# Exponentials of four slots in one instruction, their exponents formed by TensorE from split halves and scaled identities; the carry moved from the forward transform into the kernel spectrum

## The chip, the cores and the metric

One Trainium2 chip, one of its cores. The metric is the device time of the slowest (here the only) core in microseconds, lower is better. "Time" is that of a whole run; "span" is the length of one profiled execution, about 1.8 us less in the two profiled runs (171.17 and 169.4 before, 176.92 and 175.1 after). The engines are called PE (TensorE), DVE (VectorE), ACT (ScalarE), POOL (GpSimd) and SP (SyncE, which only issues transfers here). In the profile's names `AR` is the on-chip working memory (SBUF) and `ps` is PSUM, the memory into which PE writes its products; an evacuation is the copy of such products from PSUM to SBUF. u is the input, F1 the first of four forward matrices, `eye` and `rest` two parts of the constants. The granted clock is the share of full speed that the profile shows TensorE to have been given.

## The reference, cut to what matters

```python
def reference(A_u, ..., gate_w):
    g = sigmoid((x * gate_w).sum(-1, keepdims=True))
    a = _A_ref(x, ...)          # long convolution, 512 channels of 2048 steps
    b = _B_ref(x, ...)          # two routed rows through a small gated MLP
    return g * a + (1 - g) * b

def _A_ref(u, A_re, A_im, B_re, B_im, C_re, C_im, log_dt, Dskip):
    dt = exp(log_dt)[:, None]
    logdA = dt * (A_re + 1j * A_im)                     # 512 x 128
    P = exp(logdA[:, :, None] * l[None, None, :])       # l = 0 .. 2047
    K = einsum("dn,dnl,dn->dl", Cc, P, dB).real
    y = irfft2(rfft2(pad(u)) * rfft2(pad(K)))           # the convolution by FFT
    return y + u * Dskip
```

What the change touches is P: the kernel splits l into a sum of two numbers of steps and needs, for each of 32 "slots" (multiples of 8 steps), the real exponential exp(8 k dt A_re), besides sines and cosines of the imaginary part.

## The kernel before

The kernel is a list of about 640 operations in one fixed order (`SEQ`), from which every engine gets its own queue, in order; a negative number puts an operation that either ACT or DVE can do on DVE. The 512 channels are worked in two halves of 256. Stages: exponentials, tables of complex powers (sines on ACT, products on DVE), forward transform on PE, kernel generation and kernel spectrum on PE, products of spectra on DVE, inverse on PE. The parts concerned:

```python
CB = small("cb", 1792, BF)                       # identities
DQ([(CB(0, 128, 0, (1, 128)), dr(cb_c, ...))], [], [(CB, "eye")], 32768, eng=ACT)
DQ([(CB(0, 128, 128, (1, 768)), dr(cb_c, ...))], [], [(CB, "rest")], 196608, eng=ACT)
# ...
TT(w512(AL), w512(DTB), t512(PT0), ALU.mult, ...)          # AL = dt * A_re, fp32, on DVE
# ...
def exps1(h, ts):                                          # 32 slots of half h, on ACT
    for s in range(32):
        AC(TP[h][1](0, 128, s * 4, (128, 64), (1, 4)), AL(0, 128, h * HC, (4, 64), (1, 4)),
           ACTF.Exp, [AL], [(TP[h][1], ("e", s))], scale=float(T1[s]), tset=ts[s % 16 // 4])
# ... forward transform of block blk: the second block also adds the first one's result (the carry)
    if blk:
        last = h.matmul(o, CB(0, 128, 640 if part == 0 else 512, (1, 128)),
                        X(0, 128, (1 - part) * 2048 + ft * 256, (8192, 2), (1, 256)), start=False, stop=True)
# ... kernel spectrum kspec(h): for each of two values of qd, block i and part: four sums of products, then an evacuation
```

The absolute value of an angle before its cosine is one of the operations that either engine can do: 1024 elements take ACT 1.37 us and DVE 0.68 us.

## Time and profile before

| | before |
|---|---|
| time, three runs | 172.05 us median (171.6 to 172.19) |
| span of the profiled run | 169.4 us |
| busy: PE / DVE / ACT | 134.3 / 153.6 / 124.8 us |
| DVE without work | 15.8 us, 4.5 of it the last output transfer |
| mean granted TensorE clock | 0.956 |

The profile has four views that matter here: the busy shares of the engines and the row of 40 slices (each digit is tenths of a slice), the busy time by stretch, the waits by engine (what the waiting instruction writes and its line, what it waited for; total us, times, longest), and the timeline of an engine, where a bracket says how long the engine stood before the instruction and for whom. Lines of the first three for this kernel are in the prediction below. The reading: DVE has work in 153.6 of 169.4 us, so a gain must take away work or idle time of DVE.

### The profile page before, as it was taken

The page shows a single profiled execution, that of the slowest core. Times are in us where ns is not written, and L with a number is a line of the kernel's source. Part 1 is how long each engine was busy: PE and PEld are TensorE (multiplying, and loading weights), DVE is VectorE, ACT ScalarE, POOL GpSimd, SP SyncE. Part 2 cuts the span into 40 slices and gives each one's busy share as a digit, 9 for nine tenths or more (in the row PEclk, how much of TensorE's full clock was granted, in tenths as well). Part 3 has the DMA queues.
Part 4 walks back from the last instruction along what each step waited for, and adds up shares of the span by engine and source line. Part 5 has one row for each costly group of instructions (what it writes and reads, how often), then busy time and mean ns, then how long its engine had stood idle before and what let it go on. Part 6 is the DMA issues. An engine that isn't in the chain of part 4 may idle for free.

```text
span 169.4 us, 4237 instructions
## 1 busy us (share of the span) xinstructions
PE 134.3 (79%) x1807; PEld 92.3 (55%) x1807; DVE 153.6 (91%) x239; ACT 124.8 (74%) x227; POOL 18.7 (11%) x26
## 2 busy tenths in 40 slices
PE   2159999999999699888606878295989899899970
PEld 1044445544674235864404657293678688788750
DVE  0769799999989999999999999998999999999980
ACT  2899995999999999999999266964637486456000
POOL 3000000000000000000050000022220402581500
PEclk9999999999999999999965999958799999999998
DMA  4999999949109720000760298039793194899996
GB/s 113 311 397 266 290 279 395 409 163 449 50 9 336 230 110 4 4 4 4 190 233 2 53 396 297 2 65 173 265 184 68 31 201 81 155 139 157 194 214 197
DMA packets 26854, 30.15 MB, mean 178 GB/s; under 512 B 10408, under 2 KB 20532, under 8 KB 26804
## 3 DMA queue, kind: packets, MB, share of 16 engines
q1 hardware_dynamic: 20050, 23.36, 42.9%
q0 software_dynamic: 4352, 5.77, 21.6%
q10 hardware_dynamic: 2434, 0.76, 1.9%
q8 instruction: 14, 0.23, 0.5%
q14 instruction: 4, 0.03, 0.1%
HBM read 19.92 MB, written 4.20 MB: 142 GB/s over the span
## 4 chain that ended last, share of the span: by engine, by line
DVE 48%; ACT 32%; PE 6%; DMA 4%; issue 4%; SPq 2%; DVEq 0%
DVE AR L403 41%; ACT AR L415 14%; ACT AR L611 5%; PE ps L773 5%; DMA AR<-c_fwd 4%; ACT AR L419 4%; ACT AR L423 4%; DVE AR L419 3%; ACT AR L607 3%; SPq L426 2%; DVE AR L410 2%; DVE AR L423 2%; ACT L221 1%; ACT L415 1%; PE ps L940 1%
## 5 line engine op out<-in xcount | busy, mean ns | idle before, releaser
L403 DVE TENSOR_TENSOR AR<-AR 128x2048 bf16<-128x2048 bf16 (+6 forms) x127 | 111.9, 928 | 1.5 <-PE ps L819 0.5
L419 ACT ACTIVATE AR<-ps 128x1024 bf16<-128x1024 f32 (+3 forms) x39 | 31.9, 844 | 16.9 <-PE ps L858 10.5
L415 ACT ACTIVATE AR<-AR 128x256 bf16<-128x256 f32 (+4 forms) x99 | 40.2, 486 | 3.1 <-DVE AR L423 2.0
L773 PE MATMUL ps<-AR 128*128 128x512 bf16 x128 | 30.4, 389 | 2.0 <-ACT AR L419 1.6
L940 PE MATMUL ps<-AR 128*128 128x256 bf16 x256 | 29.6, 273 | 1.7 <-DVE AR L403 1.7
L940 PEld LDWEIGHTS ps<-AR 128*128 128x128 bf16 x256 | 24.6, 98 | 5.6 <-DVE AR L403 2.8
L858 PE MATMUL ps<-AR 128*128 128x256 bf16 x160 | 19.8, 279 | 3.0 <-ACT AR L419 3.0
L773 PEld LDWEIGHTS ps<-AR 128*128 128x128 bf16 x128 | 12.7, 101 | 17.3 <-ACT AR L419 2.1
L429 POOL DMA_DIRECT2D AR<-AR x14 | 14.7, 1197 | 57.1 <-DVE AR L403 51.5
L819 PE MATMUL ps<-AR 128*64 128x42 bf16 x512 | 14.9, 197 | 5.9 <-DVE AR L403 3.5
L858 PEld LDWEIGHTS ps<-AR 128*128 128x128 bf16 x160 | 15.4, 100 | 6.4 <-ACT AR L419 4.4
L819 PEld LDWEIGHTS ps<-AR 128*64 128x64 bf16 x512 | 14.2, 123 | 7.7 <-DVE AR L403 4.2
L788 PE MATMUL ps<-AR 128*128 128x512 bf16 x64 | 15.6, 379 | 0.6 <-ACT AR L419 0.6
L415 ACT ACTIVATE AR<-ps,AR 128x256 bf16<-128x256 f32 x24 | 9.7, 475 | 7.0 <-PE ps L940 6.9
L611 ACT ACTIVATE AR<-AR 128x1024 bf16<-128x1024 int16 (+1 forms) x14 | 14.5, 1050 | 0.1
L423 DVE TENSOR_SCALAR AR<-AR 128x256 int32<-128x256 f32 (+3 forms) x45 | 13.2, 337 | 0.6 <-ACT AR L611 0.4
L836 PE MATMUL ps<-AR 128*32 128x128 bf16 (+1 forms) x96 | 7.3, 420 | 7.3 <-ACT AR L419 7.3
L419 DVE CAST AR<-ps 128x1024 bf16<-128x1024 f32 (+2 forms) x11 | 11.2, 1035 | 1.3 <-PE ps L773 1.3
L993 ACT ACTIVATE AR<-AR 128x512 bf16<-128x512 bf16 x15 | 9.8, 714 | 1.4 <-DMA AR<-xp 1.4
L757 POOL DMA_INDIRECT xp<-AR x1 | 1.7, 1722 | 82.7 <-DVE AR L407 82.7
L836 PEld LDWEIGHTS ps<-AR 128*32 128x32 bf16 x96 | 4.6, 122 | 9.8 <-ACT AR L419 8.3
L788 PEld LDWEIGHTS ps<-AR 128*128 128x128 bf16 x64 | 5.8, 97 | 7.0 <-ACT AR L419 0.7
(59 smaller groups left out, 111.7 us busy)
## 6 DMA issues: line engine op xcount, KB each, us to landing
AR<-AR POOLq DMA_DIRECT2D x8, 512.0 KB, 4.8
AR<-c_ksp SPq DMA_DIRECT2D x5, 512.0 KB, 5.2
AR<-in_A_u_dram SPq DMA_DIRECT2D x2, 1024.0 KB, 6.6
AR<-c_fwd SPq DMA_DIRECT2D x4, 512.0 KB, 8.6
AR<-xp SPq DMA_DIRECT2D x2, 1024.0 KB, 7.3
AR<-c_inv SPq DMA_DIRECT2D x2, 1024.0 KB, 8.5
AR<-in_B_w_up_dram SPq DMA_DIRECT2D x2, 896.0 KB, 9.3
AR<-in_B_w_gate_dram SPq DMA_DIRECT2D x1, 1792.0 KB, 12.4
```

Of the source, the lines that this page charges most:

```text
L403: return P.op(DVE, lambda h: h.tensor_tensor(out=o, in0=a, in1=b, op=op), rd, wr, cost=tt_cost(o, a, b), **k)
L415: return P.op(ACT, lambda h: h.activation(out=o, in_=a, func=func, scale=scale, bias=bias), rd, wr, cost=0.185 + nel(o) * 0.833e-3 + (0.09 ...
L419: return P.op((ACT, DVE), (lambda h: h.activation(out=o, in_=a, func=ACTF.Copy), lambda h: h.tensor_copy(o, a)), rd, wr, cost=(0.185 + n * ...
L423: return P.op((ACT, DVE), (lambda h: h.activation(out=o, in_=a, func=ACTF.Copy, scale=c), lambda h: h.tensor_scalar(out=o, in0=a, scalar1= ...
L429: P.op(POOL, lambda h: h.dma_start(o, i, accum_op=ALU.add), rd, wr, cost=1.4, nbytes=nbytes, dma=True, tag="sum")
L611: return x.activation(out=so(2), in_=lo, func=ACTF.Sin, scale=-SC16 if m else SC16, bias=HPI(0, 128, 0, (1, 1)) if m else 0.0)
L773: last = h.matmul(o, F[ft](0, 128, ((par * 4 + st) * 2 + part) * 128, (1, 128)), U(0, 128, (blk * 8 + st * 2 + par) * D, (1, D)), start=(i ...
L788: last = h.matmul(o, F[ft](0, 128, ((4 + st) * 2 + part) * 128, (1, 128)), UN(0, 128, st * D, (1, D)), start=False, stop=(st == 3 and blk ...
L819: last = hh.matmul(pb(64 * ct, 64, (g - b0) * 42, (1, 42)), TP[h][1 - part](0, 128, g * 128 + ct, (2, 64)), TQ[h][1 - part](0, 128, g * 84 ...
L836: last = hh.matmul(pb(32 * g, 32, c4, (256, njg), (4, 64)), lw, KA[h](0, 128, c4 // 2 + 2 * (base[0] + g), (8, njg), (42, 64)), start=True ...
L858: last = hh.matmul(pb(0, 128, n * 256, (1, 256)), KPU[u](0, 128, tau * 128, (1, 128)), KC[h](0, 128, jg * 256, (1, 256)), start=(k == 0), ...
L940: last = hh.matmul(pb(0, 128, e * 256, (1, 256)), GH[q](0, 128, ((par * 2 + part) * 2 + c // 2) * 512 + (2 * t2 + e) * 128, (1, 128)), X(0 ...
```

## The change

Intent: an ACT instruction has a fixed cost beside the cost per element (404 ns for 256 elements, 1017 ns for 1024 in the rows that the prediction shows), so fewer and larger exponentials are cheaper. An exponential here carries one scale per instruction, so PE multiplies the exponents by 8k with scaled identity matrices and leaves four slots side by side in PSUM. A single bf16 operand is taken to be too coarse, so the exponent is split into a high and a low bf16 half and both products are summed in PSUM. Slots whose k is twice, four times (and so on) an odd k reuse the odd one's PSUM with a scale of 2, 4, 8, 16. The first half's identities are built by DVE, the second half's are loaded (512 KB). Secondly, the carry leaves the forward transform and is added in the kernel spectrum. `SEQ` was newly scheduled for all of it.

```diff
-DQ([(CB(0, 128, 0, (1, 128)), ...)], [], [(CB, "eye")], 32768, eng=ACT)
+DQ([(CB(0, 128, 0, (1, 336)), ...)], [], [(CB, "eye")], 86016, eng=ACT)
 ...
+for a, n in ((0, 4), (4, 12)):                   # identities of the first half, on DVE
+    TT(WD8[0](0, 128, 128 * a, (128, n), (1, 128)), CB(0, 128, 0, (0, n), (1, 128)),
+       CB(0, 128, 320 + a, (1, n), (0, 128)), ALU.mult, [(CB, "eye")], [(WD8[0], a)])
+TT(w512(ALH), w512(DTB), t512(PT0), ALU.mult, ...)         # high half, bf16
 TT(w512(AL), w512(DTB), t512(PT0), ALU.mult, ...)
+TT(f512(ALL), f512(AL), f512(ALH), ALU.subtract, ...)      # low half, bf16
 ...
 def exps1(h, ts):
-    for s in range(32):
-        AC(... one slot of 256 elements, scale=float(T1[s]) ...)
+    if h == 1:
+        DMA([(WD8[1](0, 128, 0, (1, 2048)), w8_c[:, :])], [], [WD8[1]], 524288)
+    parts = ([(1, (0, 1, 2, 3)), (2, (0, 1, 2, 3)), (4, (0, 1)), (4, (2, 3)), (8, (0, 1)), (16, (0,))],
+             [(1, (0, 1, 2, 3)), (2, (0, 1, 2, 3))], [(1, (0, 1, 2, 3))], [(1, (0, 1, 2, 3))])
+    for t in range(4):                           # four groups of four slots
+        pb = pe[h][t % 2]                        # two PSUM buffers in turn
+        # 4 x 2 matmuls: WD8[h] times ALH, then times ALL, summed
+        P.op(PE, mm, [ALH, ALL, (WD8[h], 4 if t else 0)], [pb.buf], cost=0.9)
+        for m, ix in parts[t]:
+            AC(... len(ix) slots from pb ..., ACTF.Exp, ..., scale=float(m), tset=ts[0])
 ...
-    if blk: last = h.matmul(o, CB(...), X(...), start=False, stop=True)       # forward: the carry
 ...
+    if i:                                                                     # kernel spectrum
+        last = hh.matmul(pb(0, 128, n * 256, (1, 256)), CB(0, 128, 640 if part == 0 else 512, (1, 128)),
+                         KK[h](0, 128, (1 - part) * 2048 + tau % 8 * 256, (1, 256)), start=False, stop=True)
 ...
-SEQ = ...   # the order of before
+SEQ = ...   # a new order of all operations
```

## The prediction

> **What bounds the kernel now.** I read the page first (busy shares, then the 40 slices), then the busy time by stretch, then the waits of VectorE, then the groups by form. The first lines say which engine can bound at all:
>
> ```profile
> PE 134.3 (79%) x1807; PEld 92.3 (55%) x1807; DVE 153.6 (91%) x239; ACT 124.8 (74%) x227; POOL 18.7 (11%) x26
> DVE  0769799999989999999999999998999999999980
> ACT  2899995999999999999999266964637486456000
> ```
>
> VectorE (DVE) is at 9 nearly everywhere after the first slices. ScalarE (ACT) is as full, but only in the first half: from about 90 us on it has room. The busy time by stretch puts numbers on it; the columns are time, length, and busy us of PE, weight loads, DVE, ACT, POOL:
>
> ```profile
> 0.00:5.30 5.30, 1.64 (x9) 0.87 (x9) 0.00 (x0) 1.88 (x2) 1.61 (x9) 1.00 0.55 166
> 5.30:29.00 23.70, 18.57 (x90) 9.02 (x91) 20.83 (x35) 21.06 (x50) 0.00 (x0) 1.00 1.13 318
> 29.00:86.00 57.00, 50.68 (x915) 29.70 (x913) 55.75 (x108) 56.40 (x105) 1.19 (x1) 1.00 0.46 158
> 86.00:109.20 23.20, 12.92 (x130) 9.93 (x130) 23.01 (x30) 16.61 (x23) 1.25 (x3) 0.85 0.44 160
> 109.20:164.90 55.70, 50.49 (x666) 42.80 (x666) 54.03 (x69) 28.82 (x51) 14.69 (x14) 0.94 0.80 145
> 164.90:169.40 4.50, 0.00 (x0) 0.00 (x0) 0.00 (x0) 0.00 (x0) 0.00 (x0) 0.86 0.69 200
> ```
>
> So the 169.4 us span is 153.6 us of DVE work and 15.8 us of DVE idleness: 5.3 before its first instruction, 2.9 up to 29 us, 1.3 up to 86 us, 0.2 up to 109 us, 1.7 up to its end, and 4.5 of output transfer. The chain of waits names ACT from 29 to 86 us and DVE afterwards, but in the ACT part DVE lacks only 1.25 us of 57. Both are full; relieving ACT alone lets DVE gain at most that. The DVE waits confirm how little there is to win:
>
> ```profile
> DVE AR L403 <- ACT AR L415: 5.3, 1, 5.3
> DVE AR L419 <- PE ps L550: 1.3, 1, 1.3
> DVE AR L419 <- PE ps L773: 1.3, 1, 1.3
> ```
>
> The first is the head (DVE waits for the exponential that makes dt); the other two are the early waits for transposed parameters and the first forward product. Everything else is under 0.6 us.
>
> **What the Trainium skill says.** "ScalarE: Activation LUTs", section What ACT_TABLE_LOAD costs: an ACTIVATE has a fixed part (186 ns with immediates) plus 0.833 ns per element, and back-to-back ones overlap by about 93 ns. The trace agrees: 404 ns for 256 elements, 1017 for 1024, and 20 exponentials issued in 6.13 us, 307 ns apart. Covering four slots with one instruction saves the fixed part only. The same section measures a table load at about 1283 ns, exactly what the trace has. "Vector Engine (DVE) Microarchitecture Reference", section 5.1 Performance modes: a two-source operation that reads one element again and again as an operand runs at one element per cycle. The scaled identities are built so; no row here has this form, so I price it at the one-element rate that the trace shows for fp32 operands. "Perfetto Trace Analysis", section Identifying the Most-Contended Engine: improve the engine with the highest occupancy. That is DVE here, and the change is aimed at ACT.
>
> **The change part by part.** The rows that carry the prices:
>
> ```profile
> L415 ACT ACTIVATE AR<-AR 128x256 bf16<-128x256 f32 x82 | 25.7, 404 | 0.9 <-DVE AR L403 0.8
> L419 ACT ACTIVATE AR<-ps 128x1024 bf16<-128x1024 f32 x24 | 23.8, 1017 | 10.7 <-PE ps L858 10.5
> L419 DVE CAST AR<-ps 128x1024 bf16<-128x1024 f32 x8 | 9.6, 1216 | 1.3 <-PE ps L773 1.3
> L607 DVE TENSOR_SCALAR AR<-AR 128x1024 int32<-128x1024 int32 x9 | 6.2, 684 | 0.0
> L403 DVE TENSOR_TENSOR AR<-AR 128x512 f32<-128x512 f32 x3 | 2.0, 689 | 0.1
> L994 DVE TENSOR_SCALAR AR<-AR 128x512 bf16<-128x512 bf16 x1 | 0.4, 353 | 0.0
> ```
>
> I counted instructions per engine in the two built programs, since the new schedule also moves work between engines.
>
> *Exponentials on ACT.* 64 of 256 elements go, at 0.307 us apart: -19.7 us. In come 12 of 1024 (about 0.93 apart), 6 of 512 (0.51) and 2 of 256 (0.3): +14.9. Net -4.8 us. Two of six table loads go: -2.6.
>
> *ACT work moved.* Out: ten scalings of u (0.61 apart): -6.1. In: two evacuations of 1024 and one of 504 (+2.4), the absolute values of the angles, three more of 1024 and one fewer of 768 (1.36 and 1.07: +3.0), small ones +1. ACT sum about -7 us, of which about -3 before 86 us.
>
> *DVE.* New: the identities, 512 and 1536 elements (0.69, and 1.75 extrapolated from 689 ns at 512 and 1218 at 1024): +2.4; the high half of the exponents from PSUM +0.68; the low half (fp32) +0.69. Gone to ACT: two evacuations of 1024 (-2.43), one of 504 (-0.67), angle steps (-2.05 +0.55, and one scaling -0.3), small copies (-0.84). Come from ACT: ten scalings of u at 0.353: +3.5. Sum +1.5 us; less 0.07 overlap for six more instructions, about **+1.2 us**. DVE busy becomes about 154.8.
>
> *PE.* 64 new matmuls of 256 columns at about 0.11 us: +7. The carry leaves the forward transform, 24 matmuls of 512 columns at 0.217: -5.2; it enters the kernel spectrum, 32 of 256: +3.5. Total +5.3 us, but the forward stretch, where PE was full from 20 to 50 us, loses 5.2 and receives only the 3.5 of the first half's exponents and part of the second's. PE is not the bound in sum, 140 of 169.
>
> *Head.* Three transfers are issued on ACT's queue before the table load instead of five (each about 0.5 us), so dt is there about 1 us earlier. But the identity now sits in the third and larger transfer (86 KB, not 32 KB), behind a 512 KB load on the other queue. The identity landed at about 4.1 us before (issued 1.3, 0.39 to issue, 2.4 to landing); I put it at 4.7. The 2.4 us of building then fills DVE's former idle time, but delays the first exponents to about 8.3 us from 6.0.
>
> *Early waits.* u's load is ahead of three of the four forward matrices now, so the forward transform starts near 10.5 instead of 12.3, and both 1.3 us waits should vanish. Against that, exponents come later and ACT's first stretch to the sines is 9 exponentials, 10 from PSUM, two scalings and a table load, about 14 us, ending near 22.3, so the sines end near 24, as DVE arrives for the first at 21.7: I put 2.0 us of waits there (2.9 before).
>
> *Kernel spectrum.* The second block waits for the evacuation of the first of the other part: about 1 us per quarter and half. DVE has some 21 us of products of the first half to do meanwhile, including eleven u scalings put there, and the second half's spectrum is there about 21 us after its kernel generation starts (17.3 us in the trace for the first piece, from 109.2 to 126.5, plus some 4). Just hidden; +0.9 us as an allowance.
>
> *Sum for the span:* busy 154.8 + head 4.7 + early 2.0 + later 3.1 + 0.9 + output 4.5 = 170.0, against 169.4. But the scheduler that ordered it had more freedom on ACT, and I take off 1.2 us for angle and evacuation waits that its order removes: about 168.8. The run's time was 2.65 us over the profiled span before (172.05 - 169.4), so **171.4 us**.
>
> **Rivals.**
> (a) *ACT was the limit and its 7 us come out of the time*: the chain from 29 to 86 us speaks for it. Against it stands DVE's 55.75 of 57 us there. To gain 7 us DVE would have to lose work or idleness it doesn't have: 154.8 + 4.5 output + about 4.5 head + 2 is 165.8 of span, 168.4 of time, only if every other wait vanished. Small chance.
> (b) *A new wait takes over*: the second half's identities come by a 512 KB transfer into the place of a forward matrix, so it cannot start before that matrix was last used; a load of this size took 5.2 to 8.6 us to land. If PE and ACT stand for it 2 to 4 us, in the stretch where ACT is full, the time is 173 to 176. About five us of matmuls lie in between, so mostly hidden.
> (c) *The serial kernel spectrum binds*: 1 us per link, eight links; if DVE isn't covered, 172.5 to 174. The eleven scalings on DVE suggest that room was foreseen there.
>
> **Range and chances.** The centre is the DVE ledger; errors of 1 us each in head, early waits, spectrum and overlap give 168.8 to 174.2. Two per cent below is 168.6, which needs rival (a) nearly whole: 0.11. Two per cent above is 175.5, which needs (b) and (c) together: 0.06.
>
> **What would show it right or wrong.** DVE busy of 154 to 156 with ACT at 116 to 119; DVE's first instruction at 4.3 to 5.2 us, its 1536-element product near 1.75 us (0.95 would mean two per cycle); the two 1.3 us waits gone; a wait for sines near 22 us; idle DVE after 109 us under 3 us. Wrong if DVE stands for the kernel spectrum or sines over 3 us, or if DVE busy falls under 152.

## More of the kernel before

The start of ACT before, in its timeline (start, length, operation, output <- input, count, wait), is what the later sections compare with:

```profile
6.06 10.83 ACT L415 ACTIVATE AR<-AR 128x256 bf16<-128x256 f32 x35 [0.83 <-DVE AR L403]
...
18.20 2.00 ACT L415 ACTIVATE AR<-AR 128x1024 bf16<-128x1024 int16 x2
```

The reader is to see 35 exponentials back to back from 6.06 us and the first sines at 18.2 us.

## The result

The changed kernel takes **177.03 us** (median of 4, 176.25 to 177.84) against 171.82 us of before in the same rounds (median of 4): ratio 1.0321, 95% interval 1.0242 to 1.0401. It is slower. A ratio here is the mean time of one kernel's fast runs over the mean of the other's of the same rounds, so it is not quite the ratio of the medians. "Fast" and "slow" are two states of execution; a run that took over 1.5 per cent more than the fastest of its kernel is marked slow. The mean granted clock is 0.951 (0.956 before), so the mean clock is no explanation.

The first page of the profile after, busy us and slices:

```profile
PE 142.5 (81%) x1870; PEld 100.5 (57%) x1879; DVE 155.3 (89%) x245; ACT 117.9 (67%) x179; POOL 19.8 (11%) x28
DVE  0499959799996999999999999999999899999870
ACT  4068799999999999999999255791405567246000
```

DVE's busy time is 155.3 us and ACT's 117.9: both as predicted. The span is 175.1 and not 169.4, so DVE has 1.7 us more work and 4.0 us more idle time. The busy time by stretch, cut at DVE's first instruction (6.63 us) and its last (169.65); the columns are time, length, busy us of PE, weight loads, DVE, ACT, POOL, then clock, DMA share and GB/s:

```profile
0.00:6.63 6.63, 0.60 (x1) 0.10 (x1) 0.00 (x1) 1.88 (x2) 1.86 (x10) 1.00 0.69 215
6.63:29.00 22.37, 20.23 (x169) 12.65 (x172) 20.11 (x29) 16.93 (x27) 0.00 (x0) 1.00 1.11 287
29.00:86.00 57.00, 50.70 (x808) 29.85 (x813) 53.72 (x108) 55.92 (x83) 2.71 (x2) 1.00 0.50 174
86.00:109.20 23.20, 17.46 (x204) 13.10 (x204) 23.06 (x30) 15.67 (x21) 0.55 (x2) 0.78 0.49 168
109.20:169.65 60.45, 53.55 (x690) 44.82 (x690) 58.43 (x81) 27.51 (x49) 14.63 (x14) 0.97 0.73 130
169.65:175.10 5.45, 0.00 (x0) 0.00 (x0) 0.00 (x0) 0.00 (x0) 0.00 (x0) 0.69 0.77 217
```

Length less DVE's busy time is its idle time: 6.6, 2.3, 3.3, 0.1, 2.0 and 5.5 us. In the same stretches before it was 5.3, 2.9, 1.3, 0.2, 1.7 and 4.5. The large new item is 29 to 86 us, where ACT is still full (55.92 of 57). DVE's waits after:

```profile
DVE AR L405 <- DMA AR<-c_bf: 6.6, 1, 6.6
DVE AR L425 <- ACT AR L637: 1.8, 2, 1.4
DVE AR L421 <- PE ps L800: 1.5, 1, 1.5
DVE AR L425 <- ACT AR L417: 1.1, 3, 0.5
DVE AR L405 <- ACT AR L421: 0.7, 1, 0.7
```

L637 is the cosine, L417 the sine, L800 the forward transform. DVE now starts on the constants (6.6 us; before, it waited 5.3 us for an exponential of ACT), it still waits for the first forward product, and it has new waits for sines and cosines. The start of ACT in its timeline after:

```profile
9.62 0.42 ACT L417 ACTIVATE AR<-AR 128x256 bf16<-128x256 f32 x1 [5.53 <-DVE AR L405]
...
13.48 3.68 ACT L417 ACTIVATE AR<-ps 128x256 bf16<-128x256 f32 x6 [1.00 <-PE ps L604]
18.48 2.85 ACT L417 ACTIVATE AR<-ps 128x1024 bf16<-128x1024 f32 x3 [1.31 <-PE ps L604]
...
24.29 2.01 ACT L417 ACTIVATE AR<-AR 128x1024 bf16<-128x1024 int16 x2
```

The first exponential comes at 9.62 us (6.06 before) and the first sine at 24.29 (18.20): ACT has less to do but starts later and stands for exponents (L604 are PE's products that form them). Up to 29 us it is busy 18.8 us; before it was 22.9. So the 4.1 us saved there are idle time of ACT, and from 29 us on it is as full as before.

### The profile page after: what moved, and what is told of

Same layout as the page of the kernel before. It is cut to its first block, busy times and chain, and to the rows that moved or that the text cites.

```text
span 175.1 us, 4336 instructions
## 1 busy us (share of the span) xinstructions
PE 142.5 (81%) x1870; PEld 100.5 (57%) x1879; DVE 155.3 (89%) x245; ACT 117.9 (67%) x179; POOL 19.8 (11%) x28
## 4 chain that ended last, share of the span: by engine, by line
ACT 33%; DVE 30%; PE 28%; DMA 3%; issue 3%; ACTq 1%; DVEq 0%
DVE AR L405 23%; PE ps L964 15%; ACT AR L417 12%; PE ps L880 6%; ACT AR L633 5%; ACT AR L637 5%; ACT AR L421 5%; PE ps L800 3%; ACT AR L425 3%; DMA AR<-c_bf 3%; PE ps L604 3%; DVE AR L412 2%; DVE AR L633 2%; DVE AR L1018 2%; ACT L221 1%
## 5 line engine op out<-in xcount | busy, mean ns | idle before, releaser
L405 DVE TENSOR_TENSOR AR<-AR 128x2048 bf16<-128x2048 bf16 (+6 forms) x130 | 115.8, 932 | 8.7 <-DMA AR<-c_bf 6.6
L421 ACT ACTIVATE AR<-ps 128x1024 bf16<-128x1024 f32 (+3 forms) x42 | 34.3, 848 | 24.8 <-PE ps L880 15.3
L964 PE MATMUL ps<-AR 128*128 128x256 bf16 x256 | 29.8, 274 | 2.7 <-DVE AR L405 2.7
L800 PE MATMUL ps<-AR 128*128 128x512 bf16 x125 | 29.6, 386 | 0.5 <-ACT AR L421 0.3
L964 PEld LDWEIGHTS ps<-AR 128*128 128x128 bf16 x256 | 24.9, 98 | 6.1 <-DVE AR L405 3.2
L880 PE MATMUL ps<-AR 128*128 128x256 bf16 x160 | 25.0, 300 | 3.2 <-ACT AR L421 3.2
L417 ACT ACTIVATE AR<-AR 128x256 bf16<-128x256 f32 (+5 forms) x35 | 20.9, 643 | 5.7 <-DVE AR L405 5.5
L880 PEld LDWEIGHTS ps<-AR 128*128 128x128 bf16 x160 | 17.1, 108 | 8.1 <-ACT AR L421 4.8
L800 PEld LDWEIGHTS ps<-AR 128*128 128x128 bf16 x128 | 12.6, 100 | 14.9 <-issue 0.8
L417 ACT ACTIVATE AR<-ps 128x1024 bf16<-128x1024 f32 (+2 forms) x21 | 15.9, 834 | 2.6 <-PE ps L604 2.5
L813 PE MATMUL ps<-AR 128*128 128x512 bf16 x58 | 14.3, 379 | 2.0 <-ACT AR L421 1.6
L417 ACT ACTIVATE AR<-ps,AR 128x256 bf16<-128x256 f32 x24 | 9.6, 479 | 8.2 <-PE ps L964 8.1
L637 ACT ACTIVATE AR<-AR 128x1024 bf16<-128x1024 int16 (+1 forms) x14 | 14.8, 1067 | 0.2
L857 PE MATMUL ps<-AR 128*32 128x128 bf16 (+1 forms) x96 | 8.5, 417 | 4.3 <-ACT AR L421 3.7
L604 PE MATMUL ps<-AR 128*128 128x256 bf16 x64 | 9.0, 291 | 1.8 <-DVE AR L405 1.6
L813 PEld LDWEIGHTS ps<-AR 128*128 128x128 bf16 x64 | 5.8, 99 | 7.6 <-ACT AR L421 2.0
L421 DVE CAST AR<-ps 128x1024 bf16<-128x1024 f32 (+2 forms) x8 | 8.2, 1035 | 1.5 <-PE ps L800 1.5
L633 ACT ACTIVATE AR<-AR 128x1024 int16<-128x1024 int16 (+1 forms) x7 | 9.3, 1327 | 0.2
```

The source lines that it names most:

```text
L405: return P.op(DVE, lambda h: h.tensor_tensor(out=o, in0=a, in1=b, op=op), rd, wr, cost=tt_cost(o, a, b), **k)
L417: return P.op(ACT, lambda h: h.activation(out=o, in_=a, func=func, scale=scale, bias=bias), rd, wr, cost=0.185 + nel(o) * 0.833e-3 + (0.09 ...
L421: return P.op((ACT, DVE), (lambda h: h.activation(out=o, in_=a, func=ACTF.Copy), lambda h: h.tensor_copy(o, a)), rd, wr, cost=(0.185 + n * ...
L633: q = P.op((ACT, DVE), (lambda x: x.activation(out=lo, in_=lo, func=ACTF.Abs), lambda x: x.tensor_scalar(out=w, in0=w, scalar1=16384.0, sc ...
L637: return x.activation(out=so(2), in_=lo, func=ACTF.Sin, scale=-SC16 if m else SC16, bias=HPI(0, 128, 0, (1, 1)) if m else 0.0)
L800: last = h.matmul(o, F[ft](0, 128, ((par * 4 + st) * 2 + part) * 128, (1, 128)), U(0, 128, (blk * 8 + st * 2 + par) * D, (1, D)), start=(i ...
```

## The experiments

All kernels were correct by the comparison. The profiled runs were all in the fast state; runs in the slow state are left out of ratios, with one exception: the ratio on record for a_cos takes in a run of 176.27 us that the list of runs marks slow (its three fast runs alone give 1.016). The jobs ran on different chips, each with the kernel before in the same rounds, so kernels of different jobs are compared by their ratios. The table has what the profiles and the timed runs show; "idle" is span, or stretch, less DVE's busy time. Spans are of one execution each; executions of one version differ (a_cos: 171.4, 172.5 and 173.8 in its fast ones), so sizes are read from the ratio and places from the profile.

| kernel | ratio to before (95%) | span | DVE busy | idle 0-29 | 29-70 | 70-112 | 112 to DVE's end | output |
|---|---|---|---|---|---|---|---|---|
| before | 1 | 169.4 | 153.6 | 8.2 | 1.0 | 0.5 | 1.5 | 4.6 |
| changed | 1.032 (1.024-1.040) | 175.1 | 155.3 | 8.9 | 3.1 | 0.4 | 1.9 | 5.5 |
| a_head | 1.064 (1.058-1.069) | 179.5 | 155.6 | 11.9 | 3.1 | 0.4 | 3.0 | 5.6 |
| a_uact | 1.041 (1.038-1.044) | 177.0 | 152.9 | 9.9 | 3.1 | 1.6 | 4.4 | 5.1 |
| a_order | 1.032 (1.029-1.035) | 174.0 | 155.3 | 8.9 | 3.0 | 0.4 | 1.3 | 5.2 |
| a_nocarry | 1.041 (1.033-1.049) | 175.6 | 155.5 | 9.2 | 3.0 | 1.4 | 1.4 | 5.0 |
| a_mm | 1.052 (1.048-1.056) | 177.0 | 155.4 | 11.8 | 2.6 | 0.4 | 1.8 | 5.1 |
| a_headmm | 1.046 (1.037-1.054) | 177.0 | 155.4 | 10.6 | 2.6 | 0.4 | 2.9 | 5.1 |
| b_late | 1.011 (1.007-1.015) | 171.7 | 153.7 | 10.4 | 1.0 | 0.4 | 1.6 | 4.5 |
| b_carry | 1.011 (1.005-1.018) | 171.7 | 153.9 | 8.3 | 1.0 | 0.5 | 3.2 | 4.9 |
| b_free | 1.017 (1.010-1.023) | 171.4 | 153.7 | 8.0 | 2.5 | 1.1 | 1.6 | 4.5 |
| a_pool | none given | 175.9 | 154.3 | 10.4 | 3.0 | 0.4 | 2.6 | 5.1 |
| a_best | 1.033 (1.028-1.039) | 173.6 | 155.3 | 9.0 | 2.6 | 0.4 | 1.3 | 5.0 |
| a_all | 1.032 (1.026-1.038) | 173.8 | 153.7 | 10.8 | 2.5 | 0.4 | 1.3 | 5.2 |
| a_h1 | 1.027 (1.016-1.038) | 173.3 | 153.2 | 9.5 | 2.8 | 0.4 | 2.3 | 5.1 |
| a_free1 | 1.027 (1.019-1.034) | 173.9 | 152.9 | 10.0 | 2.6 | 0.4 | 2.7 | 5.3 |
| a_cos | 1.021 (1.013-1.029) | 171.4 | 155.8 | 7.6 | 1.2 | 0.5 | 1.3 | 5.0 |
| a_last | 1.026 (1.016-1.035) | 175.5 | 153.5 | 11.5 | 1.3 | 0.4 | 3.6 | 5.2 |
| after_rep | 1.036 (1.031-1.042) | 175.9 | 155.5 | 8.8 | 3.0 | 1.6 | 1.8 | 5.2 |
| after_cos | 1.034 (1.030-1.038) | 174.6 | 155.8 | 9.8 | 1.7 | 0.4 | 1.6 | 5.2 |

The theories at the outset: **HEAD** (the late start of ACT passes through to the end), **LEDGER** (more work on DVE in the second half, scalings of u that could be on ACT), and **PE** (TensorE's order near 125 us makes it the bound afterwards). The carry was the fourth suspect. The operations that the diffs name by number are 48, 55, 58, 60: exponent products of groups t0 to t3 of the first half; 170, 171: first two groups of eight products of the forward transform; 499: first group of the inverse; 480, 482: kernel spectrum of the second half.

### a_head: identity and parameters before the large matrix

```diff
-queue of SP: F1 (512 KB), Dskip, A_im, A_re, B_im, C_im, ...; queue of ACT: log_dt, rest, eye
+queue of SP: Dskip, A_im, A_re, B_im, C_im, ..., F1; queue of ACT: log_dt, eye, rest
```

> The changed kernel with its first transfers in another order: the transfer that holds the identity before the other constants on ACT's queue, the decay parameters before the first 512 KB forward matrix. Theory HEAD (the 6.6 us in which VectorE waits for the identity delays the exponents, and ScalarE, full from 18 to 80 us, passes the delay on): the first VectorE instruction at about 4.2 us, the end of the second tables about 2.3 us earlier than 111.4, time about 174.7. Rival TAIL (the end is set after 111 us by PE's order and by the work on VectorE there, so what comes early only waits): within 0.7 us of the changed kernel, 176.5.

Measured: 181.51 us, slower than the changed kernel. DVE did start at 3.27 us and ACT at 6.50, but the input u now landed later, and the exponents of t1 stood on PE behind 16 forward products that waited for it:

```profile
14.84 5.95 PE L800 MATMUL ps<-AR 128*128 128x512 bf16 x16 [3.98 <-DMA AR<-in_A_u_dram]
20.63 1.91 PE L604 MATMUL ps<-AR 128*128 128x256 bf16 x16
```

So the first sine came at 27.52 us. The identity itself, the same 86 KB, landed 1.9 us after its issue, where it had taken 4.9 in the changed kernel behind the other constants and the 512 KB matrix: its size is not what delayed it. HEAD in this simple form fell; what it showed is that exponents and forward products share PE's one queue.

### a_uact: ten scalings of u on ACT

```diff
-DVE does 11 scalings of u (512 elements) at 117 us
+DVE does 1, ACT does 10 of them in its gap at 124 to 131 us
```

> The changed kernel with ten of the eleven scalings of u that lie on VectorE put on ScalarE, into its 6.5 us of waiting at 124 to 131 us. Theory LEDGER (VectorE is full after 111 us, each us taken from it comes out of the time): VectorE busy 155.3 to about 152.6, time about 174.3. Rival PE (the end is PE's unbroken chain from 126.7 us; but this chain starts when VectorE has the first products, so it too moves by 2.9): about the same number, but then VectorE would show about 2 us of waits for PE near the end. Rival EVAC (ScalarE's later evacuations of the kernel spectrum are delayed by the scalings): 176 to 178.

Measured: 177.95 us. DVE's busy time fell as expected (152.9), but in their place it waited 2.5 us for an accumulating transfer:

```profile
122.32 8.42 DVE L405 TENSOR_TENSOR AR<-AR 128x2048 bf16<-128x2048 bf16 x9 [2.51 <-DMA AR<-AR]
```

The scalings had filled a wait. Here work moved off the busiest engine at a place where it would stand anyway gained nothing.

### a_order: inverse after the kernel spectrum

```diff
-PE: ... 499 (first inverse) 480 482 (kernel spectrum of the second half) ...
+PE: ... 480 482 499 ...
```

> The changed kernel with one matmul group moved on PE: the first group of the inverse transform after the first two groups of the second half's kernel spectrum instead of before them, where it waits 2.7 us for VectorE with the spectrum ready behind it. Theory PE (the chain from 126.7 us on PE sets the end): 3 us off, 174.0. Theory LEDGER (VectorE is full there and waits only 0.66 us for the spectrum): 0.7 us off, 176.3.

Measured: fast runs of 175.79 to 176.29 us (a fourth, 179.91, was slow), ratio 1.0322, the same as the changed kernel's 1.0321; the span was 174.0 against 175.1. In the changed kernel the queue of PE around this place reads

```profile
126.70 1.34 PE L964 MATMUL ps<-AR 128*128 128x256 bf16 x8 [2.68 <-DVE AR L405]
127.83 5.08 PE L880 MATMUL ps<-AR 128*128 128x256 bf16 x32
```

and in a_order

```profile
124.51 3.67 PE L880 MATMUL ps<-AR 128*128 128x256 bf16 x32 [0.69 <-ACT AR L421]
```

The inverse (L964) waited 2.68 us for DVE in front of a spectrum (L880) that was ready, and PE came back at a lower rate: 5.08 us for 32 products, 3.67 in a_order. "TensorE: Matmul & The Clock Gate", section Back-to-back issue gap, gives N / 2.4 + 2.5 ns as the spacing of isolated products on a warm TensorE: 109 ns for 256 columns. a_order's trace agrees, though each product here has its own weight load: 31 gaps of 109 ns and 0.27 us for the last make 3.65. DVE's wait of 0.66 us behind it went, and its idle time after 112 us fell by 0.6. So this order is worth about 0.65 us of DVE's idle time, as the ledger said (0.7; the rest of the 1.1 us between the two spans is mostly 0.3 us less at the output); the PE theory's 3 us fell, since PE then waited for DVE instead. The timed runs don't resolve 0.4 per cent.

### a_nocarry and b_carry: one part of the change each

```diff
 a_nocarry = changed kernel
-kernel spectrum: + matmul(CB, KK of the other part)    +forward: if blk: matmul(CB, X of the other part)
 b_carry = kernel before
-forward: if blk: matmul(CB, X of the other part)       +kernel spectrum: + matmul(CB, KK of the other part)
```

> The changed kernel, same schedule, with the carry put back into the forward transform: the exponents part alone. If the carry in the spectrum is what costs (serial waits, 1.75 us of matmuls in the second half's spectrum on PE's full stretch): 174 to 175.5. If the exponents part and the head are what costs: 176.5 to 178.5, since the forward transform gets 5.2 us of matmuls back in the stretch where PE and ScalarE are full.

> The kernel before with the second part of the change alone: the carry leaves the forward transform and enters the kernel spectrum; the exponentials stay as they were. Ledger: TensorE loses 1.7 us, nothing is added on VectorE, the second part's spectrum must wait for evacuations of the first: 0 to +1.5 us (171.3 to 172.8). Rival (the carry is what costs the changed kernel its 5 us): +3 us or more.

Measured: a_nocarry 177.2 us (ratio 1.0405), no better than the changed kernel. b_carry 173.56 us (1.0112). In before's schedule the carry costs DVE two waits for the evacuation of the kernel spectrum (L419):

```profile
132.04 1.23 DVE L403 TENSOR_TENSOR AR<-AR 128x2048 bf16<-128x2048 bf16 x1 [0.94 <-ACT AR L419]
133.89 1.23 DVE L403 TENSOR_TENSOR AR<-AR 128x2048 bf16<-128x2048 bf16 x1 [0.63 <-ACT AR L419]
```

(b_carry also moves one operation of the order.) So the serial spectrum binds where nothing covers it, by 1.6 us; the changed kernel's new order covers it all but 0.66 us, and taking it out there gains nothing. The carry isn't what costs the 5 us.

### a_mm and a_headmm: the exponents first on PE

```diff
 a_mm: the changed kernel, PE
-48 170 171 55 58 ... 60
+48 55 58 170 60 171
 a_headmm: the same with 60 before 170, and a_head's transfers with F1 and u before the small constants
```

> The changed kernel; only TensorE's order changes: the products that form the exponents of the other three groups of slots stand ahead of the first 16 products of the forward transform instead of among and behind them, and their exponentials follow at once on ScalarE. QUEUE theory (ScalarE is late because its exponents stand in TensorE's queue behind products that wait for the input): ScalarE's wait of 1.3 us at 18.5 us and the gap before the last exponential go, its first sine comes at 22.6 to 23.3 us instead of 24.29, all that follows to 111 us is 1.0 to 1.7 us earlier, and the time is 175.3 to 176.0. Rival (the first sines have slack, the loss is made later by the order of the rest): the first sine moves as said, the time stays within 0.4 us of the changed kernel's 177.0.

> The same, and the identity and the parameters are loaded ahead of the 512 KB forward matrix as in a_head, with the input issued before the small constants. QUEUE theory: a_head was slow (Sin at 27.5) only since its exponents stood behind products that waited for the input; with both, VectorE starts at 3.3 us, ScalarE's first exponential is at 6.5, its exponentials run nearly without a gap, the first sine is at 20 to 20.8 us (before 18.2, changed 24.3), and since the end of the table stage moved 0.7 to 1.5 us per us of the first sine in the five kernels so far, the time is 172.5 to 174. VectorE pays a wait of 2 to 3 us near 18 us for the first forward product. Rival: 176 or more.

Measured: 180.02 and 178.65 us, both slower than the changed kernel. In a_mm the first sine came at 24.95 us, later than in the changed kernel (22.6 to 23.3 was expected). In a_headmm the first sine came at 22.02 us, 2.3 us earlier than in the changed kernel (20 to 20.8 was expected), but DVE waited 5.6 us for what stood behind the exponents now, the first forward products:

```profile
22.52 1.22 DVE L421 CAST AR<-ps 128x1024 bf16<-128x1024 f32 x1 [3.38 <-PE ps L800]
25.97 1.23 DVE L421 CAST AR<-ps 128x1024 bf16<-128x1024 f32 x1 [2.23 <-PE ps L800]
```

Not all of this is the queue. In a_headmm, PE stood 2.56 us in front of the second group of exponents and then formed two groups in 3.55 us (1.91 in the changed kernel), with the forward products behind them:

```profile
14.06 3.55 PE L604 MATMUL ps<-AR 128*128 128x256 bf16 x16 [2.56 <-DVE AR L405]
```

By the kernel's text this group writes the PSUM buffer (`peb`) that has the place of the transposed parameters (`PT1`), and DVE's last read of these ended at 14.01 us. a_mm and a_best show the same 2.56 us. No run gives these exponents another buffer, so an order with the exponents first was never tried without this wait. The queue theory was half of it: one queue starts both engines, and what was put first took from the other. Before, no exponent went through PE at all.

### b_late: the kernel before with a late identity

```diff
-CB eye: 128 columns, 32 KB, second on ACT's queue; F1 after the parameters on SP
+CB eye: 336 columns, 86 KB, third on ACT's queue, behind rest; F1 (512 KB) first on SP
```

> The kernel before, with its identity brought as late as the changed kernel brings it (a transfer of 86 KB, behind the input's log step and the other constants, and the 512 KB forward matrix first on the other queue); nothing computed changes. HEAD theory (a later first exponential passes through to the end): the first exponential is at 9 us instead of 6.06, the first sine at 20.7 to 21.5 instead of 18.2, and the time is 173.3 to 174.3 (before 171.3). Rival (the start is hidden behind the forward products, since TensorE is full from 12 us on): within 0.8 us of before.

Measured: 173.19 us, ratio 1.0109. Nothing computed changed, but the whole start came later: DVE's first instruction at 8.22 us (5.34 before), the transposes of the later parameters on PE at 12.03 (10.07), the forward products at 13.71 (12.32), and the first exponentials 2.9 us later:

```profile
8.95 10.83 ACT L415 ACTIVATE AR<-AR 128x256 bf16<-128x256 f32 x35 [3.81 <-DVE AR L403]
```

DVE's idle time before 29 us rose by 2.2 us, that of all later stretches stayed, and the span rose by 2.3. So a late start of DVE and ACT together passes through to the end, a little under the 173.3 to 174.3 that was expected; the run doesn't part the two. In the changed kernel DVE itself starts only 1.3 us later than before.

### b_free: the saving of ACT without its price

```diff
-for s in range(32): AC(one slot, 256 elements, scale=float(T1[s]))
+for s in range(0, 32, 4): AC(four slots, 1024 elements, from AL repeated, scale=float(T1[s]))   # wrong values
```

> Wrong values on purpose: the kernel before, where each four exponentials of 256 elements are one of 1024 that reads the exponents from SBUF with one scale. This is the change's saving on ScalarE for nothing: no identities, no products on TensorE, no split halves, no later start, before's schedule. ScalarE's busy time falls from 124.8 to 117 to 118 us (two table loads go too), VectorE's stays at 153.6. Ledger (VectorE sets the time, so that the saving is worth only waits that it takes away before 70 us): 168.5 to 170.5 against 171. Rival (a) of the prediction (ScalarE was the limit): 166.5 or less.

Measured: 173.86 us, ratio 1.0165: slower than before, though ACT's busy time fell to 118.3 and DVE's stayed at 153.7. (The comparison passes this kernel although its exponentials are wrong on purpose, so it doesn't see them.) The stretches to 50 us:

```profile
0.00:29.00 29.00, 19.79 (x104) 9.88 (x106) 21.00 (x35) 18.29 (x26) 1.61 (x9) 1.00 1.02 283
29.00:50.00 21.00, 20.79 (x287) 12.32 (x288) 20.24 (x58) 20.68 (x31) 0.00 (x0) 1.00 0.62 239
```

ACT's 4.65 us less work before 29 us (22.94 to 18.29) gave DVE 0.17 us more (20.83 to 21.00). After that DVE lost 1.5 us between 50 and 70 us: one evacuation now stood behind eight large exponentials on ACT (the work of 32 slots; in the kernel before only 19 small ones stand ahead of it), PE waited for it, and ran its next products at about half the rate:

```profile
61.82 3.50 PE L771 MATMUL ps<-AR 128*128 128x512 bf16 x8 [2.31 <-ACT AR L417]
```

(1.90 us for the same eight before.) So the later loss comes of where the edit put the large instructions. The stretch to 50 us is the test of the saving: ScalarE was not the limit there, and its saving, free of charge, was worth 0.17 us to DVE in before's order. No run orders the kernel anew for the shorter exponentials.

### a_pool, a_best, a_all: the start mended in other ways

```diff
 a_pool: the changed kernel
-DVE: TT(WD8[0], 1536 elements)        +POOL: tensor_tensor of the same
 a_best: the changed kernel
+SP: Dskip, A_im, A_re, ..., u, F1; ACT: log_dt, eye, rest; PE: 48 55 170 58 60 171; a_order's inverse
 a_all: both
```

> The changed kernel, its 1536-element identity product on GpSimd instead of VectorE (same order otherwise). If the building of the identities is on the path at the start, VectorE's busy time falls by 1.7 us to 153.6, the first exponential comes at 7.9 us instead of 9.62, and the time falls by 1.2 to 1.9 us to about 175.3. Rival (the exponents on TensorE need this identity and GpSimd delivers it too late, or the start has slack): within 0.5 us of the changed kernel's 177.0, or slower.

> The changed kernel mended at the start in a way that gives VectorE its forward product as well: identity and parameters first, then the input, then the forward matrix; on TensorE exponents of groups 0 and 1, the first 8 forward products, exponents of groups 2 and 3, the other 8; and the inverse after the second kernel spectrum as in a_order. In a_mm and a_headmm VectorE lost 5.5 us to the forward products that I had put behind; theory: both engines start from TensorE's one queue, so only an order that serves both gains. First sine near 22 us, VectorE's waits between 18 and 29 us under 2.5 us; time 173.5 to 175. Rival (the start's transfers, the queues being full in all kernels to 29 us, set it): 176 or more.

> a_best and a_pool together. If both theories hold, 172 to 173.5: VectorE busy 153.6, its idle time at most 1.5 us above before's 15.8. If it stays at 175 or more, the start isn't where the changed kernel loses.

Measured: a_pool 177.81 and 176.06 us in its two fast runs (two were slow), medians of 176.84 for a_best and 176.9 for a_all. POOL took 3.25 us for the identity that DVE builds in 1.76. DVE's busy time fell by 1.1 in a_pool and 1.7 in a_all, and its idle time before 29 us rose by no less (8.9 to 10.4; 9.0 to 10.8): the building of the identities lies in time in which DVE would stand for PE. In a_best the first sine is 2 us earlier (22.26), and DVE still waits 5.1 us for forward products. All three theories of the start as the place of the loss gave their misses: no mend of it alone brought the median under 176.

### a_h1 and a_free1: the first half's exponents off TensorE

```diff
 a_best, exps1, half 0 only
-identities on DVE, 32 products on PE, 10 exponentials from PSUM
+a_h1: 31 exponentials of 256 from AL, as before
+a_free1: 8 exponentials of 1024 from AL (wrong values on purpose)
```

> a_best with the first half's exponentials as in the kernel before: 31 of 256 elements straight from the fp32 exponents, no identities on VectorE, no exponent products on TensorE in the start; the second half stays changed. ScalarE gets about 3 us more to do before its sines. TensorE theory (the start is slow because exponents and forward products share one queue): VectorE's wait of 5.1 us for forward products falls under 2 us, the end of the table stage comes at 111.5 to 112.5 us instead of 114.05, time 173.5 to 175 against a_best's 176.8. ScalarE theory (its length sets the start): the first sine is at 21 us or later, no gain, 176.5 or more. Third (the rest of the order): both this and a_free1 within 0.7 us of a_best.

> Wrong values on purpose: as a_h1, but the first half's exponentials are eight of 1024 elements straight from the exponents in SBUF, so that ScalarE has the change's saving and TensorE and VectorE have none of its cost in the start. TensorE theory: the same gain as a_h1, 173 to 174.5. ScalarE theory: first sine near 19 us, 2 to 3 us faster than a_best while a_h1 is not. Third: within 0.7 us of a_best's 176.8, which says that the first half isn't where the time goes.

Measured: ratios 1.0270 and 1.0265 (a_best 1.0334). The two are alike, although ACT has 2.4 us more to do before 29 us in a_h1 (22.8 and 20.4): ACT's length at the start made no difference. DVE's wait for forward products fell from 5.1 to 3.3 us in a_h1 (under 2 was expected) and to 3.8 in a_free1, and a_h1's table stage ended at 112.64 (expected 111.5 to 112.5; a_best 114.05). But the gain of the time is 0.6 per cent, where 1 to 2 were expected, the intervals overlap, and both kernels waited longer for PE at the end. And between 29 and 70 us DVE is idle as in all variants of the changed kernel: 2.5 to 3.1 us, with 1.0 before.

### a_cos, a_last, after_rep and after_cos: ScalarE's order of the angles

That idle time is mostly one wait. In the timelines of ACT and DVE, the kernel before first, then the changed one:

```profile
48.23 1.15 ACT L611 ACTIVATE AR<-AR 128x1024 bf16<-128x1024 int16 x1
49.41 0.29 DVE L423 TENSOR_SCALAR AR<-AR 128x256 int32<-128x256 f32 x1 [0.40 <-ACT AR L611]
...
51.97 1.37 ACT L633 ACTIVATE AR<-AR 128x1024 int16<-128x1024 int16 x1
53.36 1.15 ACT L637 ACTIVATE AR<-AR 128x1024 bf16<-128x1024 int16 x1
54.55 0.29 DVE L425 TENSOR_SCALAR AR<-AR 128x256 int32<-128x256 f32 x1 [1.36 <-ACT AR L637]
```

In the changed kernel the last cosine of the first half stands behind an absolute value (L633) on ACT, and DVE waits for the cosine. In the kernel before this absolute value was on ACT too, but ACT reached the cosine at 48.23 us and DVE waited 0.40 us. Now ACT reaches it 5.1 us later and DVE only 4.2. Two causes offer themselves: ACT began its sines 6.1 us later, and the new order gave it three absolute values of the first half that DVE had done (1.37 us each). The traces of the other variants speak against the first. With the changed order the sines start anywhere from 20.84 us (a_h1) to 27.52 (a_head), and this wait is 1.32 to 1.36 us in each; in before's order it is 0.41 in b_late, whose sines start 2.9 us later, and 0.40 before. The wait goes with the order, not with the late start.

```diff
 ACT  -sine a, absolute a, cosine a, sine b, absolute b, cosine b
      +sine a, sine b, absolute a, cosine a, cosine b
 DVE  +absolute b (its other form, 0.68 us)
 a_cos = a_best + this; a_last = a_h1 + this + F1 before u; after_rep = changed kernel; after_cos = changed kernel + this
```

> a_best with ScalarE's last angles of the first half in another order: both sines, then the cosines, and the absolute value of one (1.37 us on ScalarE) done on VectorE in its other form (0.68 us). Theory (ScalarE's order of the angles makes VectorE wait): the wait of 1.36 us at 53 us falls under 0.4, VectorE's idle time between 29 and 70 us from 2.6 to about 1.5, its busy time rises by 0.7, the span goes from 173.6 to 172.8 to 173.2 and the time to 176.0 to 176.5. Rival (the first half's products are late for another reason): the idle time stays at 2.3 or more, span 174 or more.

> a_h1 (first half's exponentials as before, second half's changed) with a_cos's order and the forward matrix issued before the input. Theory: PE's wait of 5.3 us for the forward matrix shortens by about 1 us, VectorE's idle time before 29 us falls from 9.5 to about 8.5 and between 29 and 70 us from 2.8 to 1.7; span 171.5 to 172.3, ratio to before 1.014 to 1.022 (a_h1 1.027). It isn't expected to beat before, since nothing in it makes VectorE's work less. Rival: ratio stays at 1.025 or more, and the loss lies after 112 us alone.

> The changed kernel once more, unaltered, as the pair of the next run on the same chip: ratio to before 1.028 to 1.036, span 174.5 to 176.

> The changed kernel with a_cos's order of the last angles of the first half and nothing else. Angle theory: the wait of 1.36 us at 53 us goes, VectorE's idle time between 29 and 70 us falls from 3.1 to 1.6 to 2.0, its busy time rises by 0.7, so the span falls by 0.5 to 1.0 us and the time is 0.3 to 0.6 per cent under that of the changed kernel in this job. Rival (a_cos's gain was the start's, which varies from run to run): no difference of the times beyond 0.2 per cent, the wait replaced by another.

Measured: the wait is gone in a_cos, a_last and after_cos, and DVE's idle time between 29 and 70 us falls from 2.6 to 1.2 (a_cos), 2.8 to 1.3 (a_last) and 3.0 to 1.7 (after_cos), for 0.3 to 0.5 us more work. a_cos is the best version of the change, with fast runs of 173.5 to 175.62 us and 1.0209. Its profiled execution, the fastest of them (171.4 us, where 172.8 to 173.2 were expected), has 15.6 us of idle time, as little as before's 15.8, and 2.2 us more work of DVE. Part of that is luck: its idle time before 29 us, which the edit doesn't touch, is 1.4 us under a_best's, as PE ran the first eight forward products in 1.89 us and not in 3.49. The edit alone (after_cos), in the same rounds as the changed kernel (after_rep, ratio 1.036 as expected), gives 177.22 against 177.61 us (means of the fast runs), 0.2 per cent where 0.3 to 0.6 were expected, and that is within the noise. The spans of these runs fall by the 1.0 us that was expected at most (means of 175.7 and 174.7). In the profiled pair 1.0 us of the gain is met by idle time before 29 us, again outside the edit. So the wait's removal is shown in the profiles; a gain in time is not. In a_last u landed too late (PE waited 5.67 us for it), and its end waited 2.8 us for PE; the expected 1.014 to 1.022 was missed at 1.0256.

No version of the change came under before's time.

## Why the prediction was wrong

**Busy times: right.** DVE 155.3 (154.8 predicted), ACT 117.9 (116 to 119). The 1536-element product took 1758 ns (1.75 us predicted), so "Vector Engine (DVE) Microarchitecture Reference", section 5.1 Performance modes, holds for the repeated operand. PE had 142.5, where the sum was 139.6.

**Head: wrong by 1.9 us** ("I put it at 4.7"). DVE's first instruction came at 6.63 us. The step doubted the 512 KB load ahead of the identity and still priced the identity almost as if it were alone. It took 4.9 us from issue to landing, 2.4 before; a_head has it in 1.9 with neither the other constants nor the matrix ahead of it. b_late shows that such a late identity costs the kernel before 1.1 per cent, though there it delays DVE by 2.9 us and here by 1.3.

**Early waits: right in sum (2.3 us, 2.0 predicted), wrong in kind.** The wait for parameters went, that for the first forward product stayed (1.5 us). What the step left out is that the exponents' products stand in PE's queue with the forward products. a_mm and a_headmm put the exponents first and DVE waited 5.5 us, in part because PE stood 2.56 us for a PSUM buffer; a_head let the forward products go first and ACT waited 7.1. a_h1 and a_free1, without these exponents on PE, have less of that wait (3.3 and 3.8 us, 5.1 in a_best) whatever ACT's length; their gain in time is within the noise.

**"I take off 1.2 us for angle and evacuation waits that its order removes": this is the step that failed most.** Nothing had been read from a view for it. The order brought such waits in: idle time from 29 to 86 us went from 1.3 to 3.3 us. With this credit the waits after 29 us were put at 2.8 us (3.1 + 0.9 - 1.2), and they were 5.4. a_cos, a_last and after_cos show that 1.3 to 1.6 us of it is one cosine that ACT reaches too late, and that both sines first and one absolute value back on DVE mend it. The prediction itself counted three more of these on ACT (+3.0 us) and treated ACT as having room, in a stretch where its own table had ACT at 56.40 of 57 us. The late start of the sines doesn't add to this wait: it is 1.32 to 1.36 us in every variant with the changed order of these angles, early start or late.

**Kernel spectrum: about right.** 0.9 us allowed, 0.66 us of wait, and a_order takes it away. Rival (c) is real in before's schedule (b_carry, 1.6 us).

**Output: 4.5 predicted, 5.5 measured.** All variants of the changed order have 5.0 to 5.6, those of before's 4.5 to 4.9. Why is open.

**Time over span.** The 2.65 us came from a median of other runs and one profiled span; in the profiled runs it is 1.8. This error was in the other direction.

The sum from the predicted span of 168.8: +0.5 busy, +1.9 head, +0.25 early waits, +1.4 later waits with the spectrum's, +0.95 output, +1.2 for the credit that did not exist: 175.0, measured 175.1.

**Rivals.** (a) is refuted to 50 us by b_free, in before's order, and by the result: 7 us less work on ACT, and no gain. (b) did not appear: the second half's identity landed 4.8 us after its issue and ACT's wait for those exponents is 0.2 us. (c) is covered above. The prediction gave 0.06 to a time above 175.5 us, by (b) and (c) together; what happened came another way and was not on the list: ACT's saving (4.1 us before 29 us) turned into ACT's own waiting for exponents, while DVE got 1.7 us more work and 4.0 us more waits. Two of the terms are shown one by one (the late identity on before, the angles in the profiles); since mends interact through the queues, a full split of the 4.0 us isn't shown.

## What to carry to other kernels

Price a saving by what the bounding engine gets of it: an experiment that takes the work away for nothing (here wrong values in the order of before) tells in one run, read stage by stage, whether the saving is worth having before a costly way to it is built. When a change routes a second stream of work through an in-order engine that starts two others, look at who stands behind whom in that queue; sums of busy time don't show it. And never credit a new schedule with waits it might remove: "Perfetto Trace Analysis", section Optimization Strategy, tells to find the gaps on the chosen engine and what blocks it, and each gap read that way (a cosine, an inverse ahead of a ready spectrum) went from the profile, where the guesses about the start gained nothing. PE's 2.56 us at the start, which the traces name too, was left.

## What the Trainium skill lacked or had wrong

- "TensorE: Matmul & The Clock Gate", section What's actually happening, has TensorE fall to half its clock after an idle window of about 3.4 us. Here eight products of 512 columns took 3.50 us (1.90 otherwise) after a gap of 2.31 us in b_free, and 32 of 256 took 5.08 (3.67) after one of 2.68 us in the changed kernel; a gap of 1.62 us before had no effect. No length of gap comes out as the limit, however: eight products of 256 took 1.76 us (1.04 otherwise) after a gap of 1.83 us before, and 1.08 after one of 2.38 us in b_free. Only small products ran ahead of these last two and of the gap in the changed kernel, so an idle window may have been longer than the gap.
- "Perfetto Trace Analysis", section Identifying the Most-Contended Engine, says which engine to improve. No page says what a saving on another engine turns into when all queues are in a fixed order: here 6.9 us less work on ScalarE came with 4.0 us more idle time on VectorE (and 1.7 us more work there), and 6.5 us less for nothing (b_free) with 1.9 us more.
- No page has the cost of a load issued ahead of a small urgent one on another queue: the identity took 4.9 us to land (86 KB, behind a 512 KB load on the other queue and 143 KB on its own) against 1.9 for the same 86 KB with neither ahead (a_head); which of the two costs more isn't separated.
